# Another engine for many elementwise and conversion steps, and another order of all steps

## The chip, the cores and the metric

The kernel runs on one core of a Trainium2 chip. The metric is the device time of one execution in microseconds (us). Five engines take part, each with a queue of its own that it works off in order: TensorE (PE, matmuls; PEld is its weight load), VectorE (DVE), ScalarE (ACT), GpSimd (POOL) and SyncE (SP), which here only issues DMAs.

## What is computed

Three stages in a row: an mLSTM layer (recurrent attention with exponential gates; 2 batches, 8 heads, 768 steps, head size 40), a gated MLP behind an RMS norm, and a second MLP. All is float32.

```python
for t in range(S):                                   # attention, per batch and head
    m_new = np.maximum(f_gate[:, :, t] + m, i_gate[:, :, t])
    f_stab = np.exp(f_gate[:, :, t] + m - m_new); i_stab = np.exp(i_gate[:, :, t] - m_new)
    C = f_stab * C + i_stab * outer(v, k);  n = f_stab * n + i_stab * k
    y[:, :, t] = sigmoid(o_gate) * (C @ q) / maximum(abs(n @ q), 1.0)
# MLP 1: x (1536 x 320), d_ff 1536
xn = x / sqrt(mean(x * x) + 1e-6) * rms_g
x = (silu(xn @ w_gate) * (xn @ w_val)) @ w_out
# MLP 2: d_ff 2048
h = x @ w_in
out = (h * clip(h + 3, 0, 6) / 6) @ w_out
```

## The kernel before

**Tiling.** The 768 steps are cut into 6 chunks of 128; each chunk goes through the attention in a chunked form (scores, decay weights, a state that is carried from half chunk to half chunk). Two batches of a chunk give 256 tokens. For MLP 1 the chunks are taken in 3 groups of two (512 tokens each); group 0 goes through its first six column blocks in two parts of 256 tokens, so that it can begin when the first chunk is done. MLP 2 has again 3 groups of 512 tokens.

**Precision.** The MLP matmuls run in a rounded form of float32 (fp32r). Each operand is split into a rounded high part and a low part, low = x - high, and three products are added up. The helper `sub` (L93) makes each low part: both of its inputs lie in SBUF. Activations: `in1_val` (L583; product with the value half on DVE, L589; high part on ACT, L592; low part by `sub`, L594, on POOL) and `in2` (L598; relu on ACT, product on DVE, L608, high part on ACT, L611, low part by `sub`, L613, on POOL). That makes 42 + 48 low parts on POOL. Weights: they arrive as 64-bit floats and are converted by `conv` (L148) in 34 pieces, each in six to eight steps: low bits, sign, scale, a merge on DVE (L177), high part, and low parts with `sub` (L191 to L200). The table `ENGINES` gives for each piece one letter per step: A (ACT), D (DVE) or P (POOL).

**Attention on SBUF alone.** Several steps read and write only SBUF and stand on POOL: `scaled_v` (L349), `scaled_k` (L359), the decay of the state in `update` (L463), the division by the denominator in `epilogue` (L481), and the gate arithmetic of the second part in `gates_a` (L231 to L243). Steps that read a matmul's result from PSUM stand on DVE or ACT, since POOL does not read PSUM here. `REM` gives the engine of 24 small copies in `to_xT` (L498).

**Order.** No loop nest sets the order. Every step is a generator that issues one piece of work up to each `yield`; the string `PLAN` (L689) is a list of words, and each word lets the generator of that name go on to its next `yield` (L766 to L772). `m`, `M`, `o` are gate, value and output matmuls of MLP 1 (group, block, part), `h` and `p` those of MLP 2, `c` a step of a weight conversion, `W` the DMA of a weight piece, `q` and `k` DMAs of attention inputs, `G` and `g` gates, `d` decay, `s`, `w`, `a`, `i`, `u` scores, weighing, values, inter-chunk product and state update, `n`, `D`, `e` sum, denominator and epilogue, `x` and `X` transposes, `E` and `F` evacuations, and `H` four matmuls on the identity whose result nobody reads (`warm_up`, L667). So PLAN is the program order of every engine's queue and of SP's DMA queue. No wait is added for the order alone; engines wait for data and free buffers.

**Buffers.** Raw weight pieces after the fourth share two buffers (`rw`), converted weights 18 (`wp`), split activations three (`gp`), and the matmul results of gate, value and h four PSUM tiles (`pmm`, `pms`).

Of the kernel before, what the change touches and what calls it, by code (L numbers as in the profile page):

```python
# [832 lines left out]
```

## Time and profile before

| | us |
|---|---|
| median of 3 runs (lowest, highest) | 485.16 (479.79, 485.73) |
| the profiled execution | 483.2 |
| its span, first to last instruction | 481.5 |
| PE busy | 453.7 |
| DVE busy | 239.2 |
| POOL busy | 211.5 |
| ACT busy | 210.5 |

What lies around the span is 483.2 - 481.5 = 1.7 us. Busy times overlap; that of PE has matmul ends that are modelled, so a busy PE is not a PE at its peak.

### The profile page before, as it was taken

What the parts mean: (1) busy time and instruction counts of PE and PEld (TensorE: products, weight loads), DVE (VectorE), ACT (ScalarE), POOL (GpSimd) and SP (SyncE); (2) the same over time, 40 slices, a digit from 0 to 9 for tenths busy, and PEclk for the clock granted to TensorE, in tenths of its full rate; (3) what the DMA queues carried; (4) which work ended last, traced back from release to release, by engine and by line L of the source; (5) the groups of instructions that cost most, each with busy time, mean ns of one, the idle gap of its engine ahead of it and who ended that gap; (6) DMA issues with size and microseconds to landing.
All of it is one profiled execution on the core that took longest, in us unless ns stands there. A gap on an engine that the chain in (4) does not pass through costs nothing.

```text
span 481.5 us, 9199 instructions
## 1 busy us (share of the span) xinstructions
PE 453.7 (94%) x3840; PEld 407.1 (85%) x3840; DVE 239.2 (50%) x374; ACT 210.5 (44%) x413; POOL 211.5 (44%) x211
## 2 busy tenths in 40 slices
PE   7995998989989899999999799999999999999996
PEld 6995897877778689988889689899899898998986
DVE  7798768887995440111265458975313212230221
ACT  4554754544553333222355375754435313541541
POOL 7465658474771533321243353463334223531632
PEclk9997999979999999999999989999999999999999
DMA  7965093554613100000031324330001000010001
GB/s 280 290 162 192 4 244 119 180 152 144 189 71 110 43 1 1 0 1 0 1 109 56 117 104 143 131 109 1 0 1 55 1 0 1 1 55 1 0 1 54
DMA packets 10809, 37.64 MB, mean 78 GB/s; under 512 B 1552, under 2 KB 3248, under 8 KB 10768
## 3 DMA queue, kind: packets, MB, share of 16 engines
q1 hardware_dynamic: 10768, 37.06, 24.4%
q8 instruction: 30, 0.49, 0.4%
q14 instruction: 11, 0.09, 0.1%
HBM read 35.05 MB, written 2.01 MB: 77 GB/s over the span
## 4 chain that ended last, share of the span: by engine, by line
PE 65%; DVE 12%; POOL 7%; issue 6%; DMA 6%; ACT 4%; DVEq 0%; ACTq 0%; POOLq 0%; SPq 0%
PE po L543 23%; PE hh L536 17%; PE val L536 7%; PE gate L536 5%; DMA raw<-in_w_in_dram 4%; PE idle L671 3%; PE gv L536 2%; POOL g L94 2%; DVE w_in L94 2%; PE att L399 2%; DMA kvo<-in_kvo_dram 2%; POOL y L481 1%; ACT raw L171 1%; PE inter L411 1%; DVE raw L177 1%
## 5 line engine op out<-in xcount | busy, mean ns | idle before, releaser
L543 PE MATMUL po<-w_out,g 128*128 128x320 f32 x1008 | 155.4, 311 | 3.3 <-POOL g L94 2.3
L543 PEld LDWEIGHTS po<-w_out,g 128*128 128x128 f32 x1008 | 149.8, 188 | 5.9 <-POOL g L94 2.6
L94 POOL TENSOR_TENSOR g<-r,g 128x512 fp32r<-128x512 f32 x48 | 63.3, 1323 | 93.5 <-ACT g L611 93.5
L536 PE MATMUL hh<-xT,w_in 128*128 128x512 f32 x384 | 90.3, 391 | 0.1
L94 POOL TENSOR_TENSOR g<-e,g 128x512 fp32r<-128x512 f32 (+1 forms) x42 | 51.5, 1226 | 86.4 <-ACT g L592 84.2
L536 PEld LDWEIGHTS hh<-xT,w_in 128*128 128x128 f32 x384 | 71.4, 188 | 14.7 <-DVE xT L510 0.6
L608 DVE SCALAR_TENSOR_TENSOR r<-r,hh 128x512 f32<-128x512 f32 x48 | 32.8, 686 | 96.5 <-ACT r L606 96.5
L536 PE MATMUL val<-xT,w_in 128*128 128x512 f32 x240 | 61.1, 402 | 2.7 <-DVE e L589 2.7
L536 PE MATMUL gate<-xT,w_in 128*128 128x512 f32 x240 | 58.9, 394 | 4.4 <-DVE e L589 2.2
L536 PEld LDWEIGHTS gate<-xT,w_in 128*128 128x128 f32 x240 | 44.5, 188 | 14.3 <-ACT e L574 2.6
L536 PEld LDWEIGHTS val<-xT,w_in 128*128 128x128 f32 x240 | 45.2, 192 | 12.2 <-DVE e L589 3.1
L611 ACT CAST g<-r 128x512 fp32r<-128x512 f32 x48 | 29.5, 620 | 52.7 <-PE po L543 45.5
L592 ACT CAST g<-e 128x512 fp32r<-128x512 f32 (+1 forms) x42 | 23.4, 557 | 57.7 <-DVE e L589 43.9
L589 DVE TENSOR_TENSOR e<-e,val 128x512 f32<-128x512 f32 x30 | 20.4, 683 | 56.4 <-PE val L536 53.1
L606 ACT ACTIVATE r<-hh,three 128x512 f32<-128x512 f32 x48 | 32.7, 684 | 30.5 <-PE hh L536 25.9
L177 DVE SCALAR_TENSOR_TENSOR raw<-raw,bits 128x640 int32<-128x640 int32 x34 | 34.1, 1012 | 6.7 <-ACT raw L171 6.5
L536 PE MATMUL gv<-xT,w_in 128*128 128x256 f32 x192 | 27.4, 300 | 1.7 <-ACT e L574 1.1
L536 PEld LDWEIGHTS gv<-xT,w_in 128*128 128x128 f32 x192 | 25.4, 204 | 2.5 <-ACT e L574 1.3
L671 PE MATMUL idle<-ident 128*128 128x128 f32 x152 | 25.3, 337 | 2.3 <-POOL ident L105 1.5
L94 POOL TENSOR_TENSOR w_in<-raw,w_in 64x128 fp32r<-64x128 f32 (+1 forms) x25 | 23.0, 920 | 9.9 <-ACT w_in L186 5.8
L574 ACT ACTIVATE e<-gate 128x512 f32<-128x512 f32 x30 | 17.8, 593 | 20.5 <-PE gate L536 14.8
L671 PEld LDWEIGHTS idle<-ident 128*128 128x128 f32 x152 | 23.6, 246 | 2.9 <-POOL ident L105 1.5
(107 smaller groups left out, 476.7 us busy)
## 6 DMA issues: line engine op xcount, KB each, us to landing
...
```

Of the source, the lines that this page charges most:

```text
L94: eng.tensor_tensor(out=out, in0=a, in1=hi.bitcast(F32), op=ALU.subtract)
L177: nc.vector.scalar_tensor_tensor(out=x, in0=hw, scalar=3, in1=y, op0=ALU.logical_shift_left, op1=ALU.bitwise_or)
L399: nc.tensor.matmul(out=ps[t, h], lhsT=fbc[c][t, b, h], rhs=v[t, h], start=True, stop=True)
L536: nc.tensor.matmul(out=ps, lhsT=w[:, wk], rhs=xT[:, hl, kk], start=(n == 0), stop=(n == len(seq) - 1))
L543: nc.tensor.matmul(out=ps, lhsT=g[:, gh, ts], rhs=w[:, wh, k % 2], start=(first and n == 0), stop=(last and n == 2))
L574: nc.scalar.activation(out=e, in_=pg, func=ACTF.Silu)
L589: nc.vector.tensor_tensor(out=e, in0=e, in1=pv, op=ALU.mult)
L592: nc.scalar.copy(out=g[:, 0], in_=e)
L606: nc.scalar.activation(out=r, in_=ps, func=ACTF.Relu, bias=three)
L608: nc.vector.scalar_tensor_tensor(out=r, in0=r, scalar=6.0, in1=ps, op0=ALU.min, op1=ALU.mult)
L611: nc.scalar.copy(out=g[:, 0], in_=r)
L671: nc.tensor.matmul(out=idle[i][:, 0:128], lhsT=ident, rhs=ident, start=True, stop=True)
```

## The change

Four tables and one switch:

- `sub` in `in1_val` and `in2`, `scaled_v`, `scaled_k`, the state decay in `update` and the division in `epilogue` go through a new helper `either`, which picks DVE where the step's name stands in the set `ON_DVE` and POOL otherwise. On DVE are now 22 of the 42 low parts of MLP 1, 26 of the 48 of MLP 2, and of the attention steps 6 of 12 `v`, 4 of 12 `l`, 6 of 10 `u`, 5 of 12 `e`.
- 7 of the 12 evacuations `E` of MLP 1 go from ACT to DVE.
- The gate arithmetic of the second part (`gates_a`, three instructions of 640 columns) goes from POOL to DVE.
- `ENGINES` and `REM` have other letters. In `ENGINES`, of 34 pieces: low bits on ACT 21 (17 before), sign on ACT 19 (16), scale on ACT 18 (21), large low parts on POOL 12 (16), small low parts on POOL 15 (8).
- `PLAN` has the same words in another order, with 48 words `H` (38 before).

The new plan begins with the gates, and loads the attention inputs `k` and `q` ahead of most early weights; all 48 `H` stand ahead of the first gate matmul (`m0.0.0`). It has more of the MLP ahead of the last two attention chunks.

```diff
+    ON_DVE = set("""
+    v0.0 l0.1 e0.0 e0.1 v1.1 u1.0 u1.1 e1.0 e1.1 M0.0.1 M0.1.1 M0.2.0 M0.2.1 M0.4.1 M0.5.0
...
+    h1.14 h1.15 h2.2 h2.3 h2.5 h2.6 h2.9 h2.15
+    """.split())
+    REM = "APDAADDDAAPPDDPPPADDPPPP"
+    def either(step, *at):
+        word = step + ".".join(str(i) for i in at if i is not None)
+        return nc.vector if word in ON_DVE else nc.gpsimd
...
-        eng = (nc.vector, nc.gpsimd)[p]
+        eng = nc.vector
...
-        nc.gpsimd.tensor_tensor(out=v, in0=v, in1=isb.to_broadcast([128, H, D1]), op=ALU.mult)
+        either("v", c, b).tensor_tensor(out=v, in0=v, in1=isb.to_broadcast([128, H, D1]), op=ALU.mult)
...
-                nc.gpsimd.tensor_tensor(out=st, in0=states[s], in1=al, op=ALU.mult)
+                either("u", c, i).tensor_tensor(out=st, in0=states[s], in1=al, op=ALU.mult)
...
-        sub(nc.gpsimd, g[:, 1], e, g[:, 0])
+        sub(either("M", gr, m, part), g[:, 1], e, g[:, 0])
...
-        sub(nc.gpsimd, g[:, 1], r, g[:, 0])
+        sub(either("h", gr, n), g[:, 1], r, g[:, 0])
...
-            nc.scalar.activation(out=x2[n], in_=ps, func=ACTF.Copy)
+            copy = nc.vector.tensor_copy if f"E{gr}.{i}" in ON_DVE else nc.scalar.copy
+            copy(out=x2[n], in_=ps)
...
-    C L0 L1 W0 W1 W2 G1 k0.0 k0.1 C k1.0 q0.0 W3 q0.1 q1.0 q1.1 W4 C W5 R G0 H1 G0 H1 G0 H1 G0 G0 G1
+    G0 L0 L1 W0 R k0.0 G1 k0.1 k1.0 q0.0 q0.1 W1 W2 W3 W4 W5 q1.0 C q1.1 C H1 C G0 H1 G0 H1 G0 H1 G0 G0 G1
...
-    c18 c18 c19 c19 a4 M0.11 c18 c19 c19 m1.0 n4.1 n4.0 e4.1 D4 e4.0 m1.1 e4.1 m1.0 e4.0 e4.1 e4.1
+    t4.1 x3.1 l4.1 t5.0 m1.0 d5.0 M0.11 l5.0 m1.1 m1.0 d5.1 l5.0 l5.1 u4 v5.0 m1.1 u4 o0.11 u4 u4 u4
```

## Rows read from the trace of the kernel before

**Rows 1.** The page's first part: busy time, share of the span, instructions.

```profile
PE 453.7 (94%) x3840; PEld 407.1 (85%) x3840; DVE 239.2 (50%) x374; ACT 210.5 (44%) x413; POOL 211.5 (44%) x211
```

**Rows 2.** Busy time by stretch: engines, granted clock, DMA share, GB/s.

```profile
0.00:47.80 47.80, 38.22 (x575) 35.95 (x576) 38.60 (x58) 24.83 (x52) 28.77 (x46) 0.93 0.72 233
47.80:107.40 59.60, 53.09 (x793) 49.39 (x791) 46.37 (x77) 30.87 (x75) 37.23 (x39) 0.94 0.49 141
107.40:151.00 43.60, 41.04 (x591) 34.20 (x586) 34.36 (x54) 21.04 (x44) 25.70 (x26) 1.00 0.46 142
...
268.00:284.00 16.00, 13.32 (x54) 10.60 (x53) 9.03 (x12) 8.36 (x15) 6.77 (x6) 0.89 0.40 133
284.00:476.70 192.70, 192.57 (x1091) 175.40 (x1090) 71.52 (x106) 84.65 (x147) 74.36 (x58) 1.00 0.10 31
476.70:481.50 4.80, 0.64 (x5) 0.37 (x3) 0.89 (x2) 0.77 (x2) 0.00 (x0) 0.99 0.39 137
```

**Rows 3.** The chain that ended last: start us, us, what it ran.

```profile
47.83 2.01 PE gv L536 x16
...
52.51 2.05 PE idle L671 x16
...
169.62 1.99 PE att L399 x64
...
441.86 17.59 PE po L543 x120
```

**Rows 4.** Timeline of PE at the two other marks of the plan.

```profile
107.41 2.11 PE L536 MATMUL gate<-xT,w_in 128*128 128x512 f32 x8
...
151.04 3.94 PE L536 MATMUL gate<-xT,w_in 128*128 128x512 f32 x16
```

**Rows 5.** Timeline, DVE and POOL side by side, 20 to 34 and 75 us.

```profile
20.66 0.68 DVE L94 TENSOR_TENSOR w_in<-raw,w_in 128x512 fp32r<-128x512 f32 x1
...
21.80 0.73 POOL L463 TENSOR_TENSOR st<-st,al 128x328 f32<-128x328 f32 x1 [1.73 <-ACT st L467]
...
29.55 0.83 DVE L177 SCALAR_TENSOR_TENSOR raw<-raw,bits 128x640 int32<-128x640 int32 x1
...
30.41 0.54 DVE L160 TENSOR_SCALAR bits<-raw 128x640 uint16<-128x640 uint16 x1
30.84 1.02 DVE L429 TENSOR_TENSOR num<-att,num 128x328 f32<-128x328 f32 x2
...
31.35 1.59 POOL L94 TENSOR_TENSOR w_out<-raw,w_out 128x640 fp32r<-128x640 f32 x1 [3.25 <-issue]
31.78 1.51 DVE L477 SCALAR_TENSOR_TENSOR y<-kvo,num 128x320 f32<-128x320 f32 x1
...
33.80 0.43 DVE L477 SCALAR_TENSOR_TENSOR y<-kvo,num 128x320 f32<-128x320 f32 x1
...
75.08 2.55 DVE L177 SCALAR_TENSOR_TENSOR raw<-raw,bits 128x640 int32<-128x640 int32 x2
...
75.65 2.56 POOL L365 TENSOR_TENSOR kvo<-kvo,last 128x320 f32<-128x320 f32 x2
```

**Rows 6.** Groups of instructions between 170 and 240 us.

```profile
L94 POOL TENSOR_TENSOR g<-e,g 128x512 fp32r<-128x512 f32 x13 | 16.8, 1289 | 46.8 <-ACT g L592 46.8
...
L589 DVE TENSOR_TENSOR e<-e,val 128x512 f32<-128x512 f32 x12 | 8.2, 686 | 49.3 <-PE val L536 46.0 <-ACT e L574 3.2
L510 DVE TENSOR_TENSOR xT<-ps_x,xT 128x384 fp32r<-128x384 f32 x3 | 1.6, 554 | 4.2 <-ACT xT L508 4.2
L489 DVE SCALAR_TENSOR_TENSOR y<-y,ss,gbc 128x320 f32<-128x320 f32 x2 | 1.1, 553 | 1.7 <-POOL ss L487 1.7
```

**Rows 7.** Groups of instructions over the whole span.

```profile
L342 DVE TENSOR_TENSOR_SCAN fbc<-fps,inject 128x512 f32<-128x512 f32 x2 | 2.4, 1216 | 0.0
...
L239 POOL TENSOR_TENSOR fi<-fi,fd 16x640 f32<-16x640 f32 x1 | 1.5, 1548 | 0.1
```

**Rows 8.** Waits over the whole span: total us, times, longest.

```profile
POOL g L94 <- ACT g L611: 93.5, 42, 11.7
```

More of the change, by code (lines that the diff above doesn't have):

```diff
@@ L364, in scaled_k @@
         kw = heads(kvos[c, b], 0, D)
-        nc.gpsimd.tensor_tensor(out=kw, in0=kw, in1=last.unsqueeze(2).to_broadcast([128, H, D]),
-                                op=ALU.mult)
+        either("l", c, b).tensor_tensor(
+            out=kw, in0=kw, in1=last.unsqueeze(2).to_broadcast([128, H, D]), op=ALU.mult)
         kws[c, b] = kvos[c, b]
@@ L480, in epilogue @@
         den = dens[c][:, b]
-        nc.gpsimd.tensor_tensor(out=y, in0=y, in1=den.unsqueeze(2).to_broadcast([128, H, D]),
-                                op=ALU.mult)
+        either("e", c, b).tensor_tensor(
+            out=y, in0=y, in1=den.unsqueeze(2).to_broadcast([128, H, D]), op=ALU.mult)
         yield
@@ L751 @@
[L751 to L754 removed]
+    PLAN = """
+    G0 L0 L1 W0 R k0.0 G1 k0.1 k1.0 q0.0 q0.1 W1 W2 W3 W4 W5 q1.0 C q1.1 C H1 C G0 H1 G0 H1 G0 G0 G1
+    G0 H1 H1 c0 G0 G1 B0 c0 t0.0 G0 G1 G1 g0 B1 g0 t0.1 d0.0 g0 v0.1 G1 t1.0 v0.0 g0 H1 l0.0 g0 d0.1
@@ new lines @@
+    w1.1 H1 l1.1 l2.0 H1 x0.0 x0.1 l2.1 c4 w2.1 x0.1 H1 x0.1 w2.0 H1 c2 W6 W7 x0.1 H1 m0.0.0 v1.1 c3
+    v2.0 M0.0.0 m0.0.0 c3 u1 l2.0 M0.0.0 M0.0.0 u1 m0.1.0 c6 c6 u1 M0.0.0 c6 u1 M0.1.0 c3 c7 c6
+    m0.2.0 m0.1.0 u1 c3 c7 M0.1.0 i1 m0.2.0 c6 c7 M0.2.0 q3.0 i1 q3.1 M0.1.0 i1 M0.1.0 a1 c7 M0.2.0
+    c7 c6 c7 c7 o0.0.0 M0.2.0 W8 b3 b3 M0.2.0 n1.0 c7 m0.3.0 n1.1 D1 W9 M0.3.0 m0.3.0 e1.0 e1.1
+    m0.4.0 e1.0 e1.1 e1.0 M0.4.0 c8 e1.1 k2.1 M0.3.0 e1.0 m0.4.0 k3.0 c8 m0.5.0 e1.1 M0.4.0 M0.3.0
+    e1.0 c8 M0.5.0 e1.1 x1.0 m0.5.0 c8 x1.1 x1.0 x1.1 x1.0 d3.0 o0.1.0 x1.1 c9 o0.2.0 M0.5.0 M0.3.0
@@ new lines @@
+    l3.0 M0.4.0 x1.0 l2.1 t2.1 o0.3.0 x1.1 c8 M0.4.0 c8 m0.0.1 c8 t3.0 M0.5.0 v2.1 M0.0.1 c9 M0.5.0
+    v3.0 m0.0.1 u2 c8 M0.0.1 l3.0 W10 M0.0.1 m0.1.1 c9 M0.0.1 c9 o0.0.1 m0.1.1 d3.1 c9 M0.1.1 c9
+    l3.1 m0.2.1 M0.1.1 u2 W11 o0.4.0 m0.2.1 c10 c10 o0.5.0 M0.1.1 u2 c10 M0.1.1 M0.2.1 u2 c10 o0.1.1
+    M0.2.1 c10 u2 m0.3.1 c10 c11 c10 c11 m0.4.1 c10 M0.2.1 c11 s3 M0.2.1 W12 m0.3.1 c11 m0.4.1
+    o0.2.1 w3.0 c11 w3.1 c11 c11 M0.3.1 M0.4.1 M0.3.1 c11 M0.3.1 i2 M0.4.1 M0.3.1 W13 M0.4.1 c12
+    m0.5.1 c12 q4.0 q4.1 M0.4.1 i2 M0.5.1 i2 m0.5.1 c12 a2 c12 c13 M0.5.1 c13 c12 M0.5.1 c13 m0.6 b4
@@ new lines @@
+    X0.1 M1.10 M1.10 m2.0 M1.11 M1.11 M1.11 m2.1 m2.0 M2.0 m2.1 o1.10 M2.0 c18 c18 M2.0 c18 o1.11
+    M2.0 M2.1 E1 E1 c18 E1 E1 W20 o2.0 M2.1 c19 M2.1 c19 m2.2 M2.1 W21 c20 c20 m2.3 m2.2 c20 c20
+    M2.2 m2.3 c21 c21 m2.4 M2.2 c20 c21 M2.2 M2.3 c21 m2.4 M2.2 c20 c20 m2.5 M2.3 c20 M2.3 W22 M2.3
+    M2.4 m2.5 m2.6 M2.4 c21 c21 c22 c22 M2.5 W23 m2.6 c22 c22 m2.7 M2.5 c22 c22 c22 X0.0 c23 M2.6
+    X0.0 X0.2 c22 c23 X0.0 M2.7 c23 W24 M2.6 c23 o2.1 o2.2 c23 M2.4 c24 c24 M2.4 c23 m2.7 o2.3 M2.5
+    M2.7 c24 W25 o2.4 M2.5 M2.6 M2.6 m2.8 c24 M2.7 M2.7 c24 c24 m2.9 c25 c24 c24 m2.8 c25 M2.8 W26
@@ new lines @@
+    p0.10 h0.12 h0.12 p0.11 h0.13 h0.13 h0.14 h0.15 X2.0 h0.14 X2.1 h0.14 h0.14 h1.0 h0.15 h0.14
+    h0.15 X2.0 h1.0 h1.1 X2.2 X2.0 h1.0 X2.0 X2.1 h1.1 X2.2 X2.3 p0.12 X2.1 h1.1 X2.2 X2.1 X2.2 h1.2
+    h0.15 h0.15 h1.3 h1.2 h1.2 h1.4 h1.5 h1.6 p0.13 p0.14 h1.0 h1.0 h1.3 p0.15 h1.1 h1.3 h1.1 h1.7
+    h1.4 h1.2 h1.4 F0 h1.2 F0 F0 h1.8 F0 F0 h1.5 F0 F0 F0 h1.5 p1.0 h1.9 h1.3 h1.3 p1.1 h1.6 h1.6
+    p1.2 h1.4 h1.4 h1.7 p1.3 h1.5 h1.7 h1.5 p1.4 h1.6 h1.8 h1.6 h1.8 p1.5 h1.7 h1.9 h1.7 h1.9 p1.6
+    h1.8 h1.8 p1.7 h1.9 h1.9 X2.3 p1.8 X2.3 X2.3 p1.9 h1.10 h1.11 h1.10 h1.10 h1.10 h1.12 h1.11
```

115 lines of the change are left out of this document (46 added, 69 removed).

## The prediction

> **What bounds the kernel now.** I read the page's busy times first. PE is busy 94% of the span and every other engine about half [rows 1], which looks like a kernel bound by PE from end to end. The busy time by stretch, read next, splits that. From 284 us on PE is busy 192.57 of 192.70 us, and its steps run without a gap: twelve matmuls of 320 columns take 17.59 / 10 = 1.76 us [rows 2, 3]. Nothing that happens on DVE or POOL there can move the end. In the first 151 us it is otherwise: part of PE's busy time there is the words H, and the rest is short matmuls at a pace that others set. So the end is the time at which PE gets its first long run of work, plus a fixed amount of matmuls. I take three marks of the plan, which stand in both plans: the first gate matmul m0.0.0, m0.6, and m1.0, the first of group 1. Before, they start at 47.83, 107.41 and 151.04 us [rows 3, 4].
>
> What sets the pace ahead of them shows in the timeline with DVE and POOL side by side. The same DVE instruction L477 takes 0.43 us by itself and 1.51 us when a POOL step of 1.59 us is under way. Two merges L177 (0.83 us alone) and two POOL multiplications (0.73 us alone) begin at 75.08 and are done at 78.21: 3.13 us for 2 x 0.83 + 2 x 0.73 = 3.12 us of work. DVE steps with an operand in PSUM are not held: two L429 take 1.02 us beside the same POOL step of 1.59 us, and twelve L589 average 0.686 us [rows 5, 6]. So POOL steps and DVE steps that touch only SBUF run one after the other, whichever engine they stand on; DVE's PSUM steps and POOL run side by side.
>
> I turn that into a measure. Count the work that a plan has ahead of a mark at undisturbed durations; take all DVE work, add POOL's, and take off what of POOL's can lie under DVE's PSUM steps: in each gap between two SBUF-only DVE steps of the plan, the smaller of POOL's and DVE's PSUM work there. Durations: merge 0.83, other conversion steps 0.54 (0.5 where the data are f32), low parts of 512 columns 0.68 on DVE and 1.29 on POOL, POOL's 640 columns 1.59, multiplications of 320 to 328 columns on POOL 0.73, scan 1.2, products from PSUM 0.69 (512 columns), 0.55 (384) and 0.5 (328), epilogue 0.43 and 0.55 [rows 5 to 7]. Shapes between are scaled by columns.
>
> For before that gives, ahead of m1.0, DVE 108.0 us (70.1 SBUF-only, 37.9 PSUM) and POOL 73.5, of which 27.3 can be covered: 108.0 + 73.5 - 27.3 = 154.2 us, against 151.0 measured. At m0.0.0 it is 30.8 + 22.3 - 5.4 = 47.7 against 47.8, at m0.6 74.1 + 51.6 - 16.2 = 109.5 against 107.4. Three marks within 2.2% make this sum the bound of the first 151 us. PE's own work to m1.0 is 99.1 us plus 38 H of four matmuls at 2.05 / 16 us, 19.5 [rows 3]: 32 us less.
>
> **The change part by part, to m1.0.** POOL loses: the three gate steps at 1.55 us (4.6) [rows 7]; 11 of 17 low parts g, 15.3 to 5.0 us; conversion low parts 17.1 to 14.7 (one 640-column and two 512-column ones less, four small ones more, these put at 0.46, between DVE's 0.3 for that size and POOL's 0.73); multiplications v, u, l, e from 39 to 16 at 0.73 us, 28.4 to 11.7 (19 go to DVE, four are put off behind m1.0); copies 0.6. In sum 73.5 - 34.6 = 38.9 us.
>
> DVE gains: the gate steps at 0.83 (2.5); the 11 low parts, four of 512 columns and seven of 256 (5.8); 19 multiplications at 0.49, scaled between 128 columns and 0.68 for 512 (9.4); copies and conversion 2.1. It loses what the new plan puts off behind m1.0, two scans and six PSUM steps (5.7). 108.0 + 14.1 = 122.1 us: 87.5 SBUF-only, 34.6 PSUM. Of the 38.9 us on POOL 25.1 lie in gaps with PSUM work, nearly two thirds, against 27.3 of 73.5. The sum is 122.1 + 38.9 - 25.1 = 135.9 us, 18.3 below before's 154.2. At m0.0.0 it is 38.1 + 12.7 - 7.4 = 43.4, at m0.6 81.3 + 26.0 - 16.2 = 91.1.
>
> PE does not take the bound over: 97.8 us to m1.0 plus 48 H at 0.51, 24.6, is 122.4. The ten added H cost 5.1 us where PE is ready and nothing where it waits; all stand ahead of m0.0.0, where PE has 14.5 + 24.6 = 39.1 us of work against 43.4, so I count them as nothing, with 5.1 as the upper end. ACT has 85.6 us to m1.0 (86.0 before). On SP, W1 to W5 move behind k and q; the same bytes go, in a stretch where the DMA engines are busy 0.72 [rows 2], and the conversions that need those weights stand late enough in the new plan; nothing, or one load's few us if not.
>
> Behind m1.0 before needs 481.5 - 151.0 = 330.5 us. After has three output steps of 1.76 already done, and the scores, values, inter product and update of one chunk still to do (6.5 us; 64 matmuls of the values are 1.99 [rows 3]): 1.2 us more. The losses in that stretch (2.7 us of PE at 268 to 284, the tail of 4.8 [rows 2]) I leave as they are: the 37 low parts moved there, the seven evacuations and the other conversion letters fall under PE's dense run. Of the low parts on DVE each takes 0.61 us less, off the path.
>
> Span: 135.9 + 330.5 + 1.2 = 467.6; with 1.7 around it **469 us**, against 483.2 for the profiled execution and 485.16 for the median.
>
> By the Trainium skill, SBUF — State Buffer, section "SBUF: two separate sides", DVE and GpSimd share a pair of SBUF ports as an exclusive lock, held for a whole instruction, by a DVE op with two SBUF inputs or in a 2-port mode against any GpSimd op. The trace agrees at 75 us (3.13 us against 3.12). Taken alone, that rule would make the lock the only bound, which is the first rival.
>
> **The rivals.** *Only the shared work counts.* SBUF-only DVE work plus POOL is 70.1 + 73.5 = 143.6 us to m1.0 before and 87.5 + 38.9 = 126.4 after. If PSUM steps always find cover, m1.0 comes at 126.4 and the end at 126.4 + 331.7 + 1.7 = 460. For it: in before the measured 151.0 lies between 143.6 and 154.2. Against it: PE and DVE need 122 us each by then, so nothing could wait. The skill's rule above gives this time. Chance 0.13.
>
> *DVE becomes the bound.* To 151 us DVE is busy 119.3 us [rows 2], so 11.3 of stretch above its 108.0, and idle 31.7. My sum leaves after only 13.8 us for both. If stretch falls with POOL's work, to 6.0, and idle time only halves, m1.0 comes at 122.1 + 6.0 + 15.9 = 144.0 and the end at 477; with less of it at up to 490. For it: DVE would be 90% loaded with work that waits in order for ACT, PE and DMAs. Against it: before, the shared port was as loaded (143.6 of 151.0) and held its pace. Chance 0.28.
>
> *Slower.* The place is DVE's queue. A low part waits for the high part on ACT; on POOL such waits come to 93.5 us over 42 [rows 8] and hold nothing but POOL. On DVE the same wait holds the PSUM products behind it, which free PE's banks. If DVE's idle time and stretch stay 43.0 us with 14.1 us more work, m1.0 comes at 165.1 and the end at 498.5. It decides once DVE saves less than 4 us of the 43. Against it: most of those POOL waits lie in the dense run, where four PSUM tiles let PE run on. Chance 0.07.
>
> **How the numbers follow.** The forecast itself, 463 to 475, has 0.52; with the first rival faster by over 2% (below 475.5, the least that a measurement of this kernel can tell from no change) has 0.65, within 2% 0.28, slower 0.07. The range, 456 to 484, leaves out the slower case, the upper part of DVE as the bound and the lowest of the first rival, together not quite 0.2.
>
> **What would show it.** Right: m0.0.0 near 43 us, m0.6 near 91, m1.0 near 136, PE dense from there; L177 and L477 nearer 0.83 and 0.43 us than before. Wrong: m1.0 at 144 or later with DVE idle in front of instructions that wait for ACT; PE idle in front of `gate` or `val` with DVE as releaser behind 151 us; or H running while data were ready.

## The result, and the profile after

The changed kernel takes 466.8 us (median of four runs, 466.74 to 468.97), beside 484.21 us for the kernel before on the same chip: a ratio of 0.967, 95% interval 0.960 to 0.974. The forecast was 469 us, with a range of 456 to 484. The profiled execution has a span of 465.0 us, against 481.5. Medians, ranges and ratios below leave out executions that took over 1.5% longer than the fastest of their kernel at a lower granted clock, three of ten of the kernel "engines only" (whose profile is one of them and isn't used) and one of ten of "40 more on VectorE".

The page's first part (busy time, share of the span, instructions) answers [rows 1]: POOL has lost 83 us of work, DVE has gained 14, PE has the same work in a shorter span.

```profile
PE 451.7 (97%) x3880; PEld 406.7 (87%) x3880; DVE 253.5 (55%) x442; ACT 210.6 (45%) x404; POOL 128.1 (28%) x152
```

Busy time by stretch of the kernel after, cut at its own marks m0.0.0, m0.6 and m1.0 (start and end us, length, then busy time and instructions of PE, PEld, DVE, ACT and POOL, granted clock, DMA share, GB/s), answers [rows 2]:

```profile
0.00:46.20 46.20, 42.47 (x630) 40.56 (x630) 35.37 (x66) 27.31 (x59) 17.61 (x38) 0.89 0.71 241
46.20:91.40 45.20, 44.03 (x702) 41.85 (x701) 39.88 (x78) 26.46 (x60) 15.49 (x18) 1.00 0.46 146
91.40:138.90 47.50, 43.71 (x447) 37.27 (x443) 38.91 (x74) 23.84 (x50) 14.77 (x16) 1.00 0.58 168
...
268.00:284.00 16.00, 15.81 (x99) 14.63 (x98) 10.46 (x16) 10.71 (x20) 6.79 (x7) 1.00 0.36 119
284.00:460.00 176.00, 176.00 (x996) 160.51 (x995) 68.85 (x110) 73.01 (x123) 37.06 (x34) 1.00 0.07 23
460.00:465.00 5.00, 1.13 (x8) 0.86 (x6) 0.98 (x2) 0.77 (x2) 0.00 (x0) 0.83 0.37 131
```

The second line is the one to look at. From m0.0.0 to m0.6 before took 59.6 us, of which PE was busy 53.09 at a clock of 0.94 [rows 2]; now it takes 45.2, of which PE is busy 44.03 at a granted clock of 1.00 (2.4 GHz). The third line is the opposite: 47.5 us against 43.6, with PE idle for 3.8 us. PE's timeline at the marks, beside [rows 4], shows the largest part of that idle time, a wait of 1.99 us in front of m1.0 itself, and ahead of m0.0.0 a block of 13 words `H` that holds PE for 5.97 us:

```profile
38.78 5.97 PE L690 MATMUL idle<-ident 128*128 128x128 f32 x52
44.59 0.38 PE L522 MATMUL ps_x<-ident,y 128*128 128x128 f32 x2
...
46.24 0.98 PE L554 MATMUL gv<-xT,w_in 128*128 128x256 f32 x6
...
91.41 0.96 PE L554 MATMUL gate<-xT,w_in 128*128 128x512 f32 x3
...
138.88 0.66 PE L554 MATMUL gate<-xT,w_in 128*128 128x512 f32 x1 [1.99 <-ACT xT L526]
```

So the marks stand at 46.2, 91.4 and 138.9 us, where the prediction had 43.4, 91.1 and 135.9, and the stretch behind m1.0 takes 465.0 - 138.9 = 326.1 us, where it had 331.7.

**Where the time went.** PE's own matmuls, without the words `H`, are the same work in every kernel here, an estimate of 419.5 us in sum; how much of it lies ahead of a mark depends on the order alone. What a stretch has beyond its matmuls I call lost: PE idle, PE at half clock, or PE with `H`. It is worked out from each kernel's one profiled execution, with the matmul durations behind the prediction's count of 99.1 us ahead of m1.0, in us by stretch (between kernels of the same order these durations drop out; between the two orders they leave about 1 us open). The first matmul of m0.0.0 in before starts at 47.48 us in the timeline; the 47.83 of [rows 3] is where the chain enters it. The table goes by 47.48.

| kernel | to m0.0.0 | to m0.6 | to m1.0 | behind m1.0 | span |
|---|---|---|---|---|---|
| before | 33.0 | 13.9 | 5.1 | 10.0 | 481.5 |
| after | 31.7 | 2.6 | 6.7 | 4.6 | 465.0 |
| order only | 33.2 | 7.3 | 6.6 | 3.8 | 470.5 |
| early steps on GpSimd | 31.3 | 3.7 | 6.2 | 5.0 | 465.5 |
| late low parts on GpSimd | 32.3 | 3.4 | 7.4 | 8.3 | 470.9 |
| old conversion letters | 36.2 | 5.7 | 5.7 | 2.6 | 469.4 |
| 13 `H` less | 35.3 | 3.4 | 4.7 | 4.7 | 467.4 |
| third raw buffer | 31.7 | 2.1 | 2.4 | 2.4 | 457.9 |
| third raw buffer, early steps on GpSimd | 31.5 | 1.9 | 2.6 | 2.3 | 457.6 |
| third raw buffer, 13 `H` less | 31.4 | 5.6 | 2.5 | 2.0 | 460.8 |
| before, third raw buffer | 33.0 | 14.0 | 8.4 | 2.9 | 477.8 |
| before, 40 more on GpSimd | 33.5 | 12.5 | 7.2 | 6.7 | 479.5 |
| before, 40 more on VectorE | 33.8 | 12.2 | 8.5 | 6.3 | 480.3 |

The gain of 16.5 us of span is 11.3 between m0.0.0 and m0.6, 5.4 behind m1.0 and 1.3 at the start, less 1.6 between m0.6 and m1.0. Of the 11.3, 5.3 are idle time of PE (6.51 us before, 1.17 after), some 3.6 half clock (0.06 of 59.6 us), and 2.05 the four words `H` that before has in this stretch [rows 3] and after has ahead of m0.0.0.

PE's own waits tell more. Waits of PE in the kernel before (engine, tile, line, what ended the wait, us in total, times, longest):

```profile
PE ps_x L504 <- DVE xT L510: 3.8, 1, 3.8
PE val L536 <- DVE e L589: 2.7, 1, 2.7
PE po L543 <- POOL g L94: 2.3, 1, 2.3
PE gate L536 <- DVE e L589: 2.2, 1, 2.2
PE gate L536 <- ACT e L574: 2.2, 1, 2.2
```

The same view of the kernel after:

```profile
PE gate L554 <- ACT xT L526: 2.0, 1, 2.0
PE idle L690 <- POOL ident L123: 1.5, 1, 1.5
PE fps L325 <- DVE fd L268: 1.3, 1, 1.3
PE sc L400 <- DVE num L447: 1.3, 1, 1.3
PE po L561 <- ACT g L610: 0.9, 1, 0.9
```

Before had five single waits of over 2 us, each of them happening once: in the order of the list they end at 42.7, 276.6, 99.3, 133.8 and 159.0 us, so that one of them, 2.3 us for a low part on POOL, lies between m0.0.0 and m0.6; the rest of the idle time there is six waits of 0.4 to 1.1 us. Three of the five were followed by half clock. Three stretches of the kernel before in which PE sat idle, each with the stretch behind it, and last what followed the waits that end at 133.8 and 159.0 (columns as above):

```profile
38.00:41.10 3.10, 0.58 (x3) 0.15 (x2) 3.01 (x5) 1.27 (x4) 2.92 (x4) 1.00 0.51 163
41.10:47.90 6.80, 5.24 (x25) 5.24 (x26) 5.29 (x6) 1.86 (x3) 2.33 (x2) 0.50 0.53 193
...
96.40:98.80 2.40, 0.56 (x4) 0.29 (x3) 2.37 (x4) 0.64 (x3) 2.04 (x2) 1.00 0.87 257
98.80:105.60 6.80, 6.34 (x82) 5.79 (x82) 5.10 (x6) 2.27 (x5) 4.96 (x6) 0.52 0.56 169
...
273.00:276.60 3.60, 0.92 (x5) 0.42 (x4) 3.46 (x5) 1.39 (x3) 1.57 (x1) 1.00 0.04 7
276.60:280.00 3.40, 3.40 (x8) 2.73 (x9) 3.05 (x4) 1.81 (x4) 2.60 (x3) 0.50 0.56 188
...
133.80:140.60 6.80, 6.79 (x94) 6.11 (x95) 6.32 (x10) 3.69 (x8) 4.48 (x6) 1.00 0.16 63
159.00:165.80 6.80, 6.80 (x62) 5.73 (x63) 3.49 (x7) 1.52 (x4) 2.47 (x4) 1.00 0.18 64
```

PE is busy for 0.6 of 3.1, 0.6 of 2.4 and 0.9 of 3.6 us, and each time the granted clock of the next 3.4 to 6.8 us is about 0.5, the lower of its two levels (1.2 GHz). Behind the two waits of 2.2 us that end at 133.8 and 159.0 it stays at 1.00, so not every such wait is paid for twice. The eight matmuls of 512 columns from 276.57 us on take 3.69 us, where the eight from 271.91 on take 1.98; so the 2.3 us wait for a low part on POOL that ends at 99.3 us is followed by up to 6.8 x 0.48 = 3.3 us more. In the kernel after, the second line of the stretches above has no such place.

### The profile page after: what moved, and what is told of

The parts are those of the page before. It is cut to its first block, busy times and chain, and to the rows that moved or that the text cites. A ratio compares the mean times of both kernels' runs of the same rounds, so it can differ in the third digit from the quotient of the medians.

```text
span 465.0 us, 9240 instructions
## 1 busy us (share of the span) xinstructions
PE 451.7 (97%) x3880; PEld 406.7 (87%) x3880; DVE 253.5 (55%) x442; ACT 210.6 (45%) x404; POOL 128.1 (28%) x152
## 4 chain that ended last, share of the span: by engine, by line
PE 67%; DVE 12%; DMA 8%; ACT 6%; issue 2%; POOL 2%; SPq 0%; ACTq 0%; DVEq 0%; POOLq 0%
PE po L561 24%; PE hh L554 19%; PE gate L554 6%; PE val L554 6%; PE idle L690 5%; DMA raw<-in_w_out_dram 5%; DMA raw<-in_w_in_dram 3%; DVE raw L195 2%; DVE g L94 2%; POOL w_in L94 1%; DMA raw<-in_w_gv_dram 1%; PE att L417 1%; PE inter L429 1%; ACT bits L182 1%; PE gv L554 1%
## 5 line engine op out<-in xcount | busy, mean ns | idle before, releaser
L554 PE MATMUL gate<-xT,w_in 128*128 128x512 f32 x240 | 61.2, 401 | 2.9 <-ACT xT L526 2.0
L554 PE MATMUL val<-xT,w_in 128*128 128x512 f32 x240 | 59.1, 392 | 0.0
L94 POOL TENSOR_TENSOR g<-r,g 128x512 fp32r<-128x512 f32 x22 | 28.5, 1298 | 108.5 <-ACT g L629 101.7
L554 PEld LDWEIGHTS gate<-xT,w_in 128*128 128x128 f32 x240 | 45.1, 191 | 13.9 <-ACT xT L526 2.3
L94 DVE TENSOR_TENSOR g<-r,g 128x512 fp32r<-128x512 f32 x26 | 18.7, 719 | 47.2 <-ACT g L629 47.1
L94 POOL TENSOR_TENSOR w_in<-raw,w_in 64x128 fp32r<-64x128 f32 (+1 forms) x37 | 27.7, 750 | 55.9 <-ACT w_in L204 23.6
L94 POOL TENSOR_TENSOR g<-e,g 128x512 fp32r<-128x512 f32 (+1 forms) x20 | 24.1, 1207 | 54.2 <-ACT g L610 40.6
L195 DVE SCALAR_TENSOR_TENSOR raw<-raw,bits 128x640 int32<-128x640 int32 x34 | 29.2, 865 | 5.6 <-ACT raw L189 5.4
L690 PE MATMUL idle<-ident 128*128 128x128 f32 x192 | 29.3, 319 | 1.5 <-POOL ident L123 1.5
L690 PEld LDWEIGHTS idle<-ident 128*128 128x128 f32 x192 | 27.5, 229 | 2.0 <-POOL ident L123 1.5
L175 ACT ACTIVATE bits<-raw 128x640 uint16<-128x640 uint16 x21 | 19.7, 937 | 13.9 <-DMA raw<-in_w_in_dram 5.6
(111 smaller groups left out, 480.3 us busy)
```

What stands on the lines that cost most here:

```text
L175: nc.scalar.activation(out=u[:, :, 0], in_=ru[:, :, 1], func=ACTF.Copy, scale=2.0 ** -13, bias=-0.49997)
L195: nc.vector.scalar_tensor_tensor(out=x, in0=hw, scalar=3, in1=y, op0=ALU.logical_shift_left, op1=ALU.bitwise_or)
L554: nc.tensor.matmul(out=ps, lhsT=w[:, wk], rhs=xT[:, hl, kk], start=(n == 0), stop=(n == len(seq) - 1))
L690: nc.tensor.matmul(out=idle[i][:, 0:128], lhsT=ident, rhs=ident, start=True, stop=True)
```

## The experiments

**Is the shared work of DVE and POOL the bound?** The prediction's sum says that work added on POOL ahead of m1.0 comes out at m1.0, unless DVE's PSUM steps cover it. To the kernel before I added 40 multiplications on POOL whose result nobody reads:

```diff
+    extra = const.tile([128, 48], F32, name="extra")
...
+            if 110 <= at < 590 and at % 12 == 0:
+                nc.gpsimd.tensor_tensor(out=extra, in0=extra, in1=extra, op=ALU.mult)
```

> The kernel before with 40 multiplications more on GpSimd, SBUF to SBUF, 128 x 48 elements on a tile that nobody else uses, one after every twelfth word of the plan between 34 us and m1.0, each about 0.36 us (14.4 us in sum). GpSimd has some 59 us idle in the first 151. Theory 'shared work': the sum to m1.0 grows from 154.3 to 165.9; m1.0 comes 8 to 12 us later, time 491 to 496. Rival 'separate queues': GpSimd takes them in its idle time; time 483 to 486.

Measured: 481.33 us, ratio 0.9935 (0.9896 to 0.9975). The steps came shorter than expected, 0.27 us where 0.36 was put, which takes the forecast for m1.0 from 8 to 12 us later to some 6 to 9. The tile's own view in that kernel gives durations (shortest, median, longest, in ns), and the window view of the first 151 us its busy times:

```profile
L773 POOL TENSOR_TENSOR extra<-extra x40: 258/267/1181, 28.8 to 148.5; 128x48 f32<-128x48 f32 x40
```

```profile
0.00:151.00 151.00, 130.69 (x1914) 117.74 (x1915) 117.62 (x188) 77.70 (x172) 106.46 (x152) 0.92 0.56 170
```

The same stretch of the kernel before:

```profile
0.00:151.00 151.00, 132.34 (x1952) 119.53 (x1952) 119.34 (x187) 76.74 (x170) 91.71 (x111) 0.95 0.55 170
```

POOL is busy 14.7 us longer (40 x 0.267 = 10.7 undisturbed), and m1.0 comes at 152.2 instead of 151.0, m0.6 at 106.5 instead of 107.4. The whole kernel isn't slower. So the amount of POOL's work, and with it the sum of POOL's and DVE's, did not bound the first 151 us.

The same 40 multiplications on VectorE ask the same of DVE's queue, the other candidate:

```diff
+    extra = const.tile([128, 48], F32, name="extra")
...
+            if 110 <= at < 590 and at % 12 == 0:
+                nc.vector.tensor_tensor(out=extra, in0=extra, in1=extra, op=ALU.mult)
```

> As pool_40_more, with the 40 multiplications of 128 x 48 elements on VectorE instead of GpSimd; some 0.2 us each, 8 us in sum (estimate from 0.31 us for 64 x 128). VectorE is busy 119 of the first 151 us. Theory 'VectorE's queue is the pace': all of its work stands in front of something, so m1.0 comes 5 to 8 us later, time 488 to 492. Rival 'chain of loads and waits': VectorE takes them in its 32 idle us, m1.0 within 2 us, time 482 to 486.

Measured: 482.73 us, ratio 1.0007 (0.9976 to 1.0038). The tile's view and the window of that kernel:

```profile
L773 DVE TENSOR_TENSOR extra<-extra x40: 174/202/1608, 29.9 to 155.3; 128x48 f32<-128x48 f32 x40
```

```profile
0.00:151.00 151.00, 128.63 (x1887) 116.10 (x1888) 128.70 (x226) 76.96 (x170) 89.77 (x112) 0.93 0.55 169
```

DVE is busy 128.7 of 151 us instead of 119.3, 85% of the stretch, m0.6 comes at 106.5 and m1.0 at 153.5, 2.5 us later, and the time is the same. Neither queue was the bound by the amount of its work. The collisions themselves are there: single steps of 0.27 and 0.20 us took up to 1.18 and 1.61. They cost the kernel no time here.

**Engines without the order, order without the engines.** First, the kernel before with all of after's engine choices and its own `PLAN`:

```diff
+    ENGINES = """
+    AADAPP AADADD AAAADP AADDPD AAAADP ADAADD DAAADD AADADP DAAADD AADADD DDAADP DAAAPP DDDDPD
...
+    REM = "APDAADDDAAPPDDPPPADDPPPP"
...
-        sub(nc.gpsimd, g[:, 1], e, g[:, 0])
+        sub(either("M", gr, m, part), g[:, 1], e, g[:, 0])
...
```

> The changed kernel's engines (ON_DVE, ENGINES, REM, gate steps on VectorE) in the old order of PLAN. Theory 'shared work': the sum to m1.0 is DVE 128.8 + POOL 40.4 - 13.7 that can lie under PSUM steps = 155.4 us, against 154.2 for before and 135.9 for the changed kernel; so m1.0 comes near 152 us as before and the time is 480 to 486, although POOL has 33 us less to do. Rival 'POOL was too slow': with 33 us off POOL, m1.0 comes 8 us or more earlier and the time is 476 or less. Rival 'the new order does it': also no change, so this run alone does not tell it from the first.

Measured: 485.37 us (483.74 to 490.75), ratio 1.0073 (1.0025 to 1.0122). All the engine choices that take 83 us off POOL in after make this kernel no faster at all. The time is also what the prediction's sum gave for it (480 to 486).

Then the new `PLAN` with the engines, letters and gates of before, here as an edit of after:

```diff
     ENGINES = """
-    AADAPP AADADD AAAADP AADDPD AAAADP ADAADD DAAADD AADADP DAAADD AADADD DDAADP DAAAPP DDDDPD
...
+    AAAADP DADADD AADAPP DDDAPD AAAADP DAAAPD AAAAPD ADAAPD AAAADD DDADDD DADAPP DAADDD DDDAPD
...
     ON_DVE = set("""
-    v0.0 l0.1 e0.0 e0.1 v1.1 u1.0 u1.1 e1.0 e1.1 M0.0.1 M0.1.1 M0.2.0 M0.2.1 M0.4.1 M0.5.0
...
     """.split())
-    REM = "APDAADDDAAPPDDPPPADDPPPP"
+    REM = "PAAAAPAPADPADDAAPPDAADPA"
...
-        eng = nc.vector
+        eng = (nc.vector, nc.gpsimd)[p]
```

> The new PLAN with the old engines (low parts, multiplications and gate steps on GpSimd, old ENGINES and REM). Theory 'shared work': the sum to m1.0 is DVE 102.3 + POOL 70.6 - 25.2 = 147.6 us, 6.6 below before's and 11.7 above the changed kernel's; m1.0 comes at 144 to 149 us and the time is 472 to 479. Rival 'the new order does it': within 2 us of the changed kernel, 465 to 469.

Measured: 472.61 us (471.21 to 473.17), ratio 0.9791 (0.9742 to 0.984). The order alone gives 10.8 us, against 17.4 for the whole change. That, too, lies where the sum had it (472 to 479; m1.0 at 144 to 149, and it came at 144.9). In the table it takes the loss to m0.6 from 13.9 to 7.3 and that behind m1.0 from 10.0 to 3.8: PE's two waits there, 2.7 and 2.2 us, are gone and one of 0.5 is left. That the order does it all falls as well: the engine choices together give the rest, but only under this order.

**Which engine changes count.** The 33 early steps of `ON_DVE` (`v`, `l`, `u`, `e` and the low parts of group 0) back on GpSimd, the rest as after:

```diff
     ON_DVE = set("""
-    v0.0 l0.1 e0.0 e0.1 v1.1 u1.0 u1.1 e1.0 e1.1 M0.0.1 M0.1.1 M0.2.0 M0.2.1 M0.4.1 M0.5.0
-    M0.5.1 M0.6 M0.7 M0.8 M0.9 M0.11 E0.1 E0.2 v2.0 v2.1 u2.1 v3.0 v3.1 l3.1 u3.0 u3.1 e3.0 M1.1
...
+    E0.1 E0.2 E1.1 E1.2 E2.0 E2.2 E2.3 M1.1 M1.10 M1.3 M1.6 M2.1 M2.11 M2.2
```

> The changed kernel with the 33 steps of ON_DVE that stand ahead of or around m1.0 (12 low parts M0, all v, l, u, e) back on GpSimd; conversion letters, gate steps and order stay. VectorE has 15 us less to m1.0 (107.0), GpSimd 24 us more (63.1, of which 29.0 can be covered). Theory 'shared work': the sum is 141.1, 5.2 more than the changed kernel's; m1.0 at 142 to 146 us instead of 138.9, time 469 to 474. Rival 'VectorE's own queue is the bound': m1.0 comes earlier than 138.9 and the time falls below 466.

Measured: 464.81 us (463.02 to 467.22), ratio 0.9622 (0.9564 to 0.9679), so not slower than after; m1.0 at 139.0 us against 138.9. The prediction's sum wanted both later; neither came. These moves are worth nothing that can be measured.

The 36 late low parts (`M1`, `M2`, `h`) back on GpSimd:

```diff
     ON_DVE = set("""
...
-    M1.3 M1.6 M1.10 E1.1 E1.2 l4.1 u4.1 l5.0 M2.1 M2.2 M2.4 M2.6 M2.9 M2.11 E2.0 E2.2 E2.3 h0.0
-    h0.1 h0.2 h0.3 h0.5 h0.6 h0.7 h0.11 h0.13 h0.14 h0.15 h1.0 h1.1 h1.4 h1.8 h1.10 h1.11 h1.13
-    h1.14 h1.15 h2.2 h2.3 h2.5 h2.6 h2.9 h2.15
+    E0.1 E0.2 E1.1 E1.2 E2.0 E2.2 E2.3 M0.0.1 M0.1.1 M0.11 M0.2.0 M0.2.1 M0.4.1 M0.5.0
...
```

> The changed kernel with the 36 low parts of groups 1 and 2 of the first MLP and of the second MLP back on GpSimd. Theory: they lie under a dense TensorE; the time is that of the changed kernel, 466 to 468. Rival 'the shorter low part counts': each is 0.6 us longer on GpSimd; if a third of that shows, 36 x 0.2 = 7 us, 474.

Measured: 471.14 us (468.05 to 472.7), ratio 0.9757 (0.9694 to 0.982): 4.3 us more than after by the medians, every run of it above the median of after, while the intervals just overlap. The table puts 3.7 us of it behind m1.0. The window of that kernel, and PE's waits from 280 us on, show one place (the window of after stands below it):

```profile
284.00:300.00 16.00, 14.31 (x82) 12.48 (x81) 10.55 (x21) 9.90 (x20) 8.55 (x8) 1.00 0.24 79
```

```profile
284.00:300.00 16.00, 16.00 (x92) 14.41 (x91) 13.39 (x26) 10.21 (x19) 2.90 (x3) 1.00 0.25 83
```

```profile
PE ps_x L520 <- DVE xT L526: 1.1, 1, 1.1
PE ps_x L520 <- POOL rem L514: 0.5, 1, 0.5
PE hh L552 <- DVE r L624: 0.5, 1, 0.5
```

POOL is busy for 8.55 of these 16 us and a copy `rem` that PE's transposes wait for stands in its queue; after is busy on PE for all of 284 to 300 us, with POOL at 2.90. These waits are 2.1 of the 3.7 us; the rest was not traced to a place. Only the 0.5 for `rem` is a wait for POOL itself, and the kernel with the early steps on GpSimd, whose late low parts stand as in after, also has a wait of 1.4 us for `xT` at 283 us. So what the prediction called off the path was probably on it, by some 4 us at most; with four runs of each it is not settled.

The conversion's letters and `REM` of before, the rest as after:

```diff
     ENGINES = """
-    AADAPP AADADD AAAADP AADDPD AAAADP ADAADD DAAADD AADADP DAAADD AADADD DDAADP DAAAPP DDDDPD
...
+    AAAADP DADADD AADAPP DDDAPD AAAADP DAAAPD AAAAPD ADAAPD AAAADD DDADDD DADAPP DAADDD DDDAPD
...
-    REM = "APDAADDDAAPPDDPPPADDPPPP"
+    REM = "PAAAAPAPADPADDAAPPDAADPA"
```

> The changed kernel with the old letters of ENGINES and REM (engines of the conversion steps and small copies); ON_DVE, gate steps and order stay. Theory 'shared work': the sum to m1.0 is 119.9 + 41.8 - 21.3 = 140.4 against 135.9, so m1.0 at 142 to 144 us, time 469 to 472. Theory 'weight ring': the conversions take part in the ring's cycle, so any steps that wait longer show there too; W19 later than 126.0 us by as much as m1.0 is. Rival 'letters do not matter': 466 to 468.

Measured: 469.81 us (467.4 to 471.15), ratio 0.9704 (0.9639 to 0.9768), 3 us more than after, well inside the two intervals; the sum had 469 to 472 (m1.0 at 142 to 144, and it came at 145.4). In the table it loses 3.1 more to m0.6 and gains 2 back behind m1.0, beside a start that was 4.5 later in that execution. A small gain from the letters is possible and not settled.

**The buffers of the raw weights.** In after the chain that ended last runs through weight DMAs. Pieces of it up to m1.0 (start us, us, what):

```profile
124.94 0.46 POOL w_in L94
...
125.47 0.47 POOL w_in L94
...
125.96 9.17 DMA raw<-in_w_out_dram
...
136.02 0.91 ACT bits L182
...
136.95 0.51 DVE raw L192
...
137.48 1.41 DVE raw L195 x2
...
138.96 1.03 DVE xT L528 x2
```

The last conversion step of one piece, on POOL, frees a raw buffer at 125.94 us; the next piece's DMA starts then and takes 9.17; its conversion follows on ACT and DVE; and the two evacuations `xT` that m1.0 needs, one on ACT (the wait of 1.99 us above) and one on DVE, stand behind these steps in the two queues. To take the wait away I gave the ring a third buffer, loaded each piece one slot earlier, and made room by allocating the four `x2` tiles of the last group later:

```diff
-    rw = ctx.enter_context(tc.tile_pool(name="rw", bufs=2))
+    rw = ctx.enter_context(tc.tile_pool(name="rw", bufs=3))
...
-    x2 = {i: const.tile([128, DM], F32, name=f"x2_{i}") for i in range(B * G1[-1][0])}
+    x2 = {i: const.tile([128, DM], F32, name=f"x2_{i}") for i in range(B * G1[1][0])}
...
-    i0 c2 c1 i0 c1 g1 H1 c2 q2.0 q2.1 H1 i0 c0 i0 c1 H1 c2 a0 c1 c4 c1 c2 c1 g1 c5 c5 g1 H1 n0.0
+    i0 c2 c1 i0 c1 g1 H1 c2 q2.0 q2.1 H1 i0 c0 i0 c1 H1 c2 W6 a0 c1 c4 c1 c2 c1 g1 c5 c5 g1 H1 n0.0
...
-    w1.1 H1 l1.1 l2.0 H1 x0.0 x0.1 l2.1 c4 w2.1 x0.1 H1 x0.1 w2.0 H1 c2 W6 W7 x0.1 H1 m0.0.0 v1.1 c3
+    w1.1 H1 l1.1 l2.0 H1 x0.0 x0.1 l2.1 c4 w2.1 x0.1 H1 x0.1 w2.0 H1 c2 W7 W8 x0.1 H1 m0.0.0 v1.1 c3
```

> The changed kernel with three instead of two buffers for raw weight pieces (the room comes from four x2 tiles that move to the later pool), and each weight load from W6 on issued one load earlier in the plan. Theory 'weight ring': in the changed kernel the loads W6 to W19 come in pairs 15 us apart (35.1 to 126.0 us), and this cycle of load and conversion is what holds m1.0 at 138.9 us. With a third buffer the cycle gets shorter: W19 some 8 us earlier, m1.0 at 130 to 136 us, time 459 to 464. Rival 'VectorE and GpSimd work': the loads are hidden anyway; m1.0 stays at 138 to 140, time 466 to 468.

Measured: 459.35 us (458.88 to 463.5), ratio 0.9512 (0.9443 to 0.9581), faster than both kernels. Its stretch from m0.6 to m1.0, which took 47.5 us in after, with 3.8 of them idle on PE:

```profile
90.80:134.00 43.20, 42.94 (x446) 37.47 (x443) 39.53 (x75) 22.38 (x47) 14.55 (x16) 1.00 0.60 171
```

PE is busy for 42.94 of 43.20 us: 4.3 of the 7.1 us of span come from here, 2.2 from behind m1.0. The ring had become after's bound between m0.6 and m1.0.

Was it the bound of before too, so that the change's gain was a better use of the ring? The same edit in the kernel before:

```diff
-    rw = ctx.enter_context(tc.tile_pool(name="rw", bufs=2))
+    rw = ctx.enter_context(tc.tile_pool(name="rw", bufs=3))
...
-    q2.1 w0.1 c2 s1 w0.0 c3 a0 c3 c4 c4 H1 c3 c5 H1 n0.0 c5 H1 c3 n0.1 b1 b1 b2 H1 b2 e0.0 c4 H1 D0
+    q2.1 w0.1 c2 s1 w0.0 c3 W6 a0 c3 c4 c4 H1 c3 c5 H1 n0.0 c5 H1 c3 n0.1 b1 b1 b2 H1 b2 e0.0 c4 H1
...
```

> The kernel before with a third buffer for raw weight pieces and each load from W6 on issued one load earlier, as in third_raw_buffer. Theory 'weight ring': in the kernel before the loads W6 to W19 (40.7 to 145.5 us) come in pairs 17 us apart, and m1.0 follows W19 by 5.5 us; with a third buffer W19 comes 5 to 10 us earlier, m1.0 at 142 to 147 us, time 474 to 479. Rival 'the queues': the order of the steps on VectorE holds m1.0 at 150 to 152 whatever the loads do, time 482 to 485.

Measured: 477.69 us (476.54 to 479.52), ratio 0.9893 (0.9847 to 0.9939). It gains 5.8 us, and behind m1.0 alone 7.1 (10.0 lost there becomes 2.9; the waits of 2.2 us at 159 us and 2.7 at 277 us are gone), while m0.6 stays at 107.5 and m1.0 comes at 154.4, in an execution whose granted clock is 0.50 from 99.1 to 116.2 us, where that of before was back at 1.00 from 106 us on. With a third buffer in both kernels the change is worth 477.7 - 459.4 = 18.3 us, as much as without. So its gain as a whole is not one of the ring. Behind m1.0 it is otherwise: there the third buffer alone takes from before what the order alone takes (2.9 and 3.8 us of loss are left), and with it in both kernels only 0.5 of the 5.4 us remains.

Finally the early steps once more, now with the ring out of the way, in case the ring had hidden them:

```diff
-    rw = ctx.enter_context(tc.tile_pool(name="rw", bufs=2))
+    rw = ctx.enter_context(tc.tile_pool(name="rw", bufs=3))
...
-    v0.0 l0.1 e0.0 e0.1 v1.1 u1.0 u1.1 e1.0 e1.1 M0.0.1 M0.1.1 M0.2.0 M0.2.1 M0.4.1 M0.5.0
...
```

> third_raw_buffer with the 33 early steps of ON_DVE (low parts M0, all v, l, u, e) back on GpSimd. With the ring relieved, what the engines carry should show if it counts at all. Theory 'VectorE's queue': 15 us less there, time 454 to 457. Theory 'shared work': the sum is 5 us larger, time 462 to 465. Rival 'neither': 458 to 461.

Measured: 459.01 us (458.64 to 461.04), ratio 0.9511 (0.9468 to 0.9555), against 0.9512 with these steps on DVE. The engine of the early steps doesn't show in the time, here either.

**The words `H`.** After with 13 of the `H` between x0.0 and x0.1 taken out:

```diff
-    x0.0 x0.0 H1 x0.0 d1.1 H1 l1.0 H1 H1 d2.0 l1.1 H1 H1 t1.1 H1 d2.1 H1 H1 t2.0 H1 w1.0 l1.0 H1
-    w1.1 H1 l1.1 l2.0 H1 x0.0 x0.1 l2.1 c4 w2.1 x0.1 H1 x0.1 w2.0 H1 c2 W6 W7 x0.1 H1 m0.0.0 v1.1 c3
+    x0.0 x0.0 x0.0 d1.1 l1.0 d2.0 l1.1 t1.1 d2.1 t2.0 w1.0 l1.0 w1.1 l1.1 l2.0 x0.0 x0.1 l2.1 c4
+    w2.1 x0.1 H1 x0.1 w2.0 H1 c2 W6 W7 x0.1 H1 m0.0.0 v1.1 c3
```

> The changed kernel without the 13 words H between the transposes x0.0 and x0.1 (52 matmuls, 5.97 us on TensorE from 38.78 us on). Theory 'H is on the path': the transposes x0.1 come 2 us earlier, m0.0.0 at 44 instead of 46.2, and the time is 464 to 465.5. Rival 'the clock': TensorE idles 3 to 5 us there, the granted clock falls to 0.5 for the first gate steps, and the time is 467 or more. Third: m0.0.0 comes earlier but the weight ring sets m1.0, time unchanged at 466 to 468.

Measured: 464.09 us (463.04, 463.49, 464.68 and 469.12), ratio 0.9612 (0.9534 to 0.9689). Three runs lie 2 to 4 us below after, the fourth, the profiled one, above it; its start came 3.6 us later at half clock. This run decides nothing. The same with the third buffer:

```diff
-    rw = ctx.enter_context(tc.tile_pool(name="rw", bufs=2))
+    rw = ctx.enter_context(tc.tile_pool(name="rw", bufs=3))
...
-    x0.0 x0.0 H1 x0.0 d1.1 H1 l1.0 H1 H1 d2.0 l1.1 H1 H1 t1.1 H1 d2.1 H1 H1 t2.0 H1 w1.0 l1.0 H1
+    x0.0 x0.0 x0.0 d1.1 l1.0 d2.0 l1.1 t1.1 d2.1 t2.0 w1.0 l1.0 w1.1 l1.1 l2.0 x0.0 x0.1 l2.1 c4
...
```

> third_raw_buffer without the 13 words H between x0.0 and x0.1. Theory 'H is on the path': m0.0.0 1 to 2 us earlier and all behind it, time 456 to 458. Rival 'the clock': half speed at the first gate steps, 459 or more.

Measured: 461.87 us (460.98 to 463.68), ratio 0.9564 (0.951 to 0.9617), 2.5 us more than with all `H` by the medians, while the runs overlap (458.88 to 463.5 with, 460.98 to 463.68 without). PE's longest wait and three stretches of that kernel:

```profile
PE ps_x L522 <- DVE xT L528: 5.6, 1, 5.6
```

```profile
40.00:46.00 6.00, 3.20 (x16) 3.21 (x16) 5.69 (x11) 3.00 (x6) 4.40 (x7) 0.50 0.37 120
46.00:91.00 45.00, 42.47 (x630) 40.31 (x629) 36.53 (x72) 25.51 (x58) 14.72 (x18) 0.96 0.41 129
...
73.50:77.00 3.50, 3.46 (x20) 3.15 (x14) 3.38 (x9) 0.97 (x3) 0.00 (x0) 0.51 0.33 88
```

Where the 13 `H` were, PE now waits 5.6 us; the clock of 40 to 46 us is 0.50, and m0.0.0 comes at 45.9 us instead of 46.1. So in front of m0.0.0 the `H` cost next to nothing, though the timeline shows PE busy with them up to the transposes. The loss to m0.6 rises from 2.1 to 5.6, nearly all of it at one place: a wait of 1.6 us of the state update `U` and the half clock from 73.5 us on. Nothing ties that place to the missing `H`, and without the third buffer the same cut gave a lower median; whether the `H` pay is not shown.

## Why the prediction was right, and where it was not

**The number.** 466.8 against 469 us, faster by 3.3%. Two errors of the terms cancel: m1.0 came 3.0 us later than 135.9, and the stretch behind it took 5.6 us less than 331.7. With the mechanism wrong, that the number came so close is in good part luck.

**The sum as the bound: wrong.** It is the step on which everything else stood. It met three marks of before within 2.2%, and m0.6 of after within 0.3 us; it also gave the times of the engines without the order, of the order without the engines and of the old letters. Still it is not what set the pace: 10.7 us more on POOL moved m1.0 by 1.2 us and the kernel not at all; 8 to 9 us more on DVE moved m1.0 by 2.5 us and the kernel not at all; the 33 early steps back on POOL, nothing, with two raw buffers or three. The step that failed is "three marks within 2.2% make this sum the bound". Three marks of one kernel grow together, so agreement at them says little of the cause. And at two of them the sum lay above the measured time (154.2 against 151.0, 109.5 against 107.4), which a bound cannot do: work that fits into less time than its sum was not all in line. A test is to add work.

**Both rivals that forecast through work fall with it.** That only the shared work counts gave 460 and the same steps as the cause; with the added work it is 143.6 + 10.7 = 154.3 us of work ahead of an m1.0 that came at 152.2. That DVE becomes the bound put m1.0 at 144 or later: DVE is busy for 114.2 of 138.9 us in after, and with 33 of its steps moved away m1.0 stays where it is. By the Trainium skill, SBUF — State Buffer, section "SBUF: two separate sides", a DVE and a GpSimd instruction that need the shared ports exclude each other for a whole instruction. The traces agree on single steps: with fewer POOL steps the merge has a mean of 865 ns instead of 1012, and the added 0.20 us steps stretched to 1.61 at worst. The page doesn't say that this sets a kernel's time, and here the sum of it didn't; it counts where PE waits for the stretched step, as the rows below show. Two of the prediction's readings are less clean than it has them: of the two L429 that run beside a POOL step only the second does (they start at 30.84, the POOL step at 31.35), and the two POOL multiplications at 75 us begin 0.57 us after the merges [rows 5]; neither changes its sum.

The merges of before and of after, by lines (total us, mean ns, idle before them):

```profile
L177 DVE SCALAR_TENSOR_TENSOR raw<-raw,bits 128x640 int32<-128x640 int32 x34 | 34.1, 1012 | 6.7 <-ACT raw L171 6.5
```

```profile
L195 DVE SCALAR_TENSOR_TENSOR raw<-raw,bits 128x640 int32<-128x640 int32 x34 | 29.2, 865 | 5.6 <-ACT raw L189 5.4
```

**What set the pace instead.** By the traces, single waits of PE, with half a clock behind some of them. The two of over 2 us that were followed by a half-clock stretch behind m0.0.0, in the kernel before (start us, us):

```profile
97.57 1.64 POOL L94 TENSOR_TENSOR g<-e,g 128x256 fp32r<-128x256 f32 x1
99.25 0.64 PE L543 MATMUL po<-w_out,g 128*128 128x320 f32 x1 [2.30 <-POOL g L94]
...
274.00 1.57 POOL L94 TENSOR_TENSOR w_out<-raw,w_out 128x640 fp32r<-128x640 f32 x1 [6.50 <-DVE w_out L198]
274.01 1.91 DVE L174 TENSOR_SCALAR raw<-raw 128x640 f32<-128x640 f32 x1
275.84 0.67 DVE L589 TENSOR_TENSOR e<-e,val 128x512 f32<-128x512 f32 x1
276.57 0.79 PE L536 MATMUL val<-xT,w_in 128*128 128x512 f32 x1 [2.68 <-DVE e L589]
```

In the first, the low part that PE waits for stands behind a division `y` on POOL and takes 1.64 us, where the same step takes 0.73 at 53.5 us. In the second, the product that PE waits for stands on DVE behind a conversion step L174 that takes 1.91 us beside a POOL step of 1.57, where it takes 0.50 at 271.1 us. So a step counts by who stands behind it, not by how much work there is. Between m0.0.0 and m0.6, where 11.3 of the 16.5 us come from, the new order alone takes 6.6 us of loss away (2.05 of it the `H` that it puts elsewhere), and 6.2 more behind m1.0. That the order gives 10.8 us and the engine choices give nothing without it is shown; which of its many moves removes which wait was not tried and stays open. So does which engine choices give the rest under it: the late low parts and the letters are candidates, and the gate steps and the evacuations `E` were not tried by themselves.

**"The losses behind m1.0 left as they are": wrong.** They fell from 10.0 to 4.6 us, most of it by the order (3.8 with the order alone).

**"Off the path" for the late low parts: probably wrong, by up to about 4 us.** PE was dense in before from 284 us, but that was before's order. In the new one, with the old engines for these steps, PE waits among others for a copy on a POOL that is three times as busy between 284 and 300 us (8.55 us against 2.90).

**Ten more `H` as nothing: not contradicted.** With the third buffer m0.0.0 moved by 0.2 us without 13 of them; without it the medians leave up to 3 us open. m0.0.0 itself was 2.8 us later than the sum had it; in the place of the missing `H` PE waits for an evacuation `xT` on DVE, and what holds that one was not traced.

**"Nothing, or one load's few us" for the weight loads: mis-sized.** The loads did come earlier, but the two-buffer ring became the next bound, 4.3 us between m0.6 and m1.0 and 7.5 us by the medians. The prediction looked at what SP issues and at the bytes, not at who frees the buffer that a load waits for.

**The signs to look for.** "m0.6 near 91" and "PE dense" behind m1.0 came true with the mechanism wrong; the signs were of the time, not of the cause. "L177 and L477 nearer 0.83 and 0.43" came true too (means of 1012 and 865 ns, 564 and 497 ns), and was not what made the kernel faster.
